# POOL and SP bound to program order, a head's loads placed nearer to their use, and two last splits on DVE

## The chip, the cores and the metric

The kernel runs on one core of a Trainium2 chip. The metric is device time in microseconds of one execution. The engines are named as in the profile: PE is TensorE (PEld its weight loads), DVE is VectorE, ACT is ScalarE, POOL is GpSimd, and SP is the engine that issues nearly all DMAs here.

## The reference

One transformer block over 2048 rows of width 576: an adaptive layer norm, attention with 32 query heads over 16 key and value heads (only the last 512 cached positions count, no mask inside them), a gated residual, a second adaptive layer norm, a SwiGLU MLP of width 4608, and a second gated residual. Cut to its core:

```python
mod = (_silu(c) @ w_mod).reshape(c.shape[0], 6, 1, -1)        # sa, ca, ga, sb, cb, gb
h = _layernorm(x) * (1 + ca) + sa
q = (h @ wq).reshape(B, Sq, Hq, Dh)...                         # 32 heads of 128
k = jnp.repeat(k_cache[:, :, Sk - W:, :], rep, axis=1)         # W = 512
v = jnp.repeat(v_cache[:, :, Sk - W:, :], rep, axis=1)
p = _softmax(jnp.einsum("bhqd,bhkd->bhqk", q, k) * Dh ** -0.5)
x = x + ga * (jnp.einsum("bhqk,bhkd->bhqd", p, v)... @ wo)
h = _layernorm(x) * (1 + cb) + sb
x = x + gb * ((_silu(h @ w1) * (h @ w3)) @ w2)
```

## The kernel before

Every float32 operand of a large product is split into a high part, rounded to the matmul's input type, and a low part, the difference. `split(hi, lo, src, eng)` does it: ACT casts (L84), then the engine `eng`, POOL or DVE, subtracts (L85). A product is then three matmuls: high by high, high by low, low by high. This split is what ACT, DVE and POOL spend much of their time on.

**Attention.** The 2048 rows form four blocks of 512. A *slot* is one head on one block; there are 128 slots, blocks 0 and 1 first, head by head, then blocks 2 and 3. The main loop runs over slots `i`, and inside over four *steps* `t`, each for 128 rows. In step t of loop i PE transposes the probabilities of slot i-1 (`turn`), makes the scores of slot i (`scores`), a quarter of the query projection of slot i+1 (`query`), and the output projection of slot i-2 (`attend_out`). After the four steps come the value products of slot i-1 (`values`). ACT takes the exponentials (L325), copies the transposed probabilities out (L336) and casts; DVE takes maxima (L319) and low halves and accumulates (L366).

**Side work during attention.** The loop calls `run(i, t)` at the end of each step (and `run(i, -1)` at the start of a slot); it emits the tasks that `at(i, t, task, ...)` registered. Those of a head: load wq (`load_in`), split it (`split_in`), load wo (`load_out`), multiply it by the gate on POOL (`gate`, L770), split it (`split_out`), load k (`load_kv`), transpose it on PE (`turn_k`), load v, split it (`split_v`). The loads of a head share a ring of three buffers with the tag `raw`. Also in these steps the weights of the MLP are prepared for a seven-product scheme (Strassen-like, ORDER and DOWN): `load_raw` (12 DMA issues, L471 and L474) and `make_set` (seven pieces per chunk f: ACT casts, L489; POOL subtracts, L490 and L491; SP stores to `wd`, L492; at n = 0 and n = 2 POOL first forms sums, L483 to L487), and `load_rows` and `make_rows` for w2. `make_rows` at n = 0 forms all the sums of a pair of row chunks on POOL, then makes its first piece out of the last of them:

```python
nc.gpsimd.tensor_mul(r, r, half_split(gates["b"]))      # L538, twice
nc.gpsimd.tensor_sub(t1, b12, b11)                      # L541
nc.gpsimd.tensor_sub(t2, b22, t1)                       # L542
nc.gpsimd.tensor_sub(t4, b21, t2)                       # L543
nc.gpsimd.tensor_sub(b12, b22, b12)                     # L544
k, x = (("p4", t4), ("p7", b12), ("p6", t2), ...)[n]
keep(x, ...)   # ACT cast L525, POOL subtraction L526, SP store to od L529
```

The prepared pieces pass through four buffers with the tag `xn`, each free again when its store has landed. There are 385 such items: 290 of them over the 232 steps of the list `early` (five items on four steps), the rest over the 128 steps of `late`. 19 of the items are `make_rows` at n = 0.

**MLP.** 72 groups (36 chunks f, each for two pairs of blocks) of seven products (`product`, L567), each with seven matmuls. `act_steps` splits the activations of a chunk pair between the products, and `down` multiplies them by the prepared rows (L645). In the last group, `plain` does four plain products per row tile instead; it needs the halves of p1 and p7, which `act_steps` splits at k = 0 and 1, and those of p4 and p2 at the end. `finish` adds partial sums on POOL (L589 to L593), `finish_first` (L600) on POOL or DVE.

**What sets the order.** Every engine executes its own queue in order. The framework's scheduler makes the queues: `tc.manual_schedule(engines=ORDERED)` keeps, for the engines in the set, the order in which the program emits its instructions; the others are ordered by the scheduler, which may move an instruction ahead of others on its engine when its inputs allow. Before, PE, DVE and ACT are in the set.

Of the kernel before, what the change touches and what calls it, by code (L numbers as in the profile page):

```python
# [24 lines left out]
HQ, HKV, DH = 32, 16, 128  # L25
# [5 lines left out]
EPS = 1e-5  # L31
PB, QB, RB, HB = 4, 1, 3, 7

ORDERED = {mybir.EngineType.PE, mybir.EngineType.DVE, mybir.EngineType.Activation}
SCALE = float(DH) ** -0.5


# [1 line left out]
def tile_block(  # L39
# [14 lines left out]
    nc = tc.nc  # L54
# [27 lines left out]
    def split(hi, lo, src, eng):  # L82

        nc.scalar.copy(hi, src)  # L84
        eng.tensor_sub(lo, src, hi.bitcast(F32))  # L85
# [210 lines left out]
    hT, wqs, keys, vals, wos = {}, {}, {}, {}, {}  # L296
# [277 lines left out]
    def split_act(d, k, x, eng):  # L574
        tags = ("ah", "al") if k in ("p7", "p4", "p6") else ("kv", "kv")
        hi, lo = [pool.tile([P, SB], F32R, tag=t, name=f"a{t}", bufs=8 if t == "kv" else 3) for t in tags]
        split(hi, lo, x, eng)
        halves[d, k] = hi, lo
# [82 lines left out]
    def act_steps(g, k):  # L661

        d, j = divmod(g, 2)
        x, pool_sub = acts[d], nc.gpsimd.tensor_sub
        if d == 2 * G - 1 and j == 1:
            if k in (0, 1):
                split_act(d, ("p1", "p7")[k], x[0, k], nc.gpsimd)
            elif k in (5, 6):
                split_act(d, ("p4", "p2")[k - 5], x[1, 6 - k], nc.vector)
        elif j == 0 and d and k < 4:  # L670
            o = acts[d - 1]
            if k == 0:
                split_act(d - 1, "p6", o[0, 0], nc.gpsimd)
            elif k == 1:
                split_act(d - 1, "p5", o[0, 1], nc.gpsimd)
            elif k == 2:
                split_act(d - 1, "p2", o[1, 0], nc.gpsimd)
                pool_sub(o[1, 0], o[1, 0], o[0, 0])
            elif k == 3:
                split_act(d - 1, "p3", o[1, 0], nc.gpsimd)  # L680
                del acts[d - 1]
        elif j == 1:
            if k == 0:
                x["s3"] = pool.tile([P, SB], F32, tag="ql", name="s3", bufs=QB)
                pool_sub(x["s3"], x[0, 0], x[0, 1])
            elif k == 1:
                split_act(d, "p7", x.pop("s3"), nc.gpsimd)
            elif k == 4:
                split_act(d, "p1", x[0, 0], nc.gpsimd)
            elif k == 5:  # L690
                split_act(d, "p4", x[1, 1], nc.vector)
            elif k == 6:
                nc.gpsimd.tensor_add(x[0, 1], x[0, 1], x[1, 1])
                pool_sub(x[0, 0], x[0, 1], x[0, 0])
# [6 lines left out]
    def mlp():  # L701

        for g in range(len(groups)):
# [9 lines left out]
            for k, name in enumerate(ORDER):  # L713
# [25 lines left out]
                elif name == "p4":  # L739
                    nc.vector.tensor_add(u0, st["x"], u0)  # L740
                    nc.vector.tensor_mul(u0, u0, st["s0"])
                act_steps(g, k)
                for _ in range(after[k]):
                    for task, *args in units:
# [9 lines left out]
    def at(i, t, task, *args):  # L754

        tasks.setdefault((i, t), []).append((task, args))
# [18 lines left out]
    for key, i in first.items():  # L775
        h, kv = key[1], (key[0], key[1] // 2)
        if i >= 2:
            at(i - 3, -1, load, wqs, key, load_in, wq, h * DH)
            at(i - 2, 1, put, wqs, key, split_in)
        at(max(i - 2, 0), -1, load, wos, key, load_out, wo, h * DH)  # L780
        at(max(i - 2, 1), 1, gate, wos, key, "a")
        at(max(i - 1, 1), 2, put, wos, key, split_out)
        if i and h % 2 == 0:
            at(i - 4, -1, load, keys, kv, load_kv, k_cache, h // 2)
            at(i - 2, -1, put, keys, kv, turn_k)
            at(i - 2, -1, load, vals, kv, load_kv, v_cache, h // 2)
            at(i - 1, 0, put, vals, kv, split_v)


# [91 lines left out]
    for c in range(3):  # L881
        i = 2 * HQ + 22 + 8 * c
# [141 lines left out]
```

## Time and profile before

| | us |
|---|---|
| median of 3 runs | 3106.66 (3104.28 to 3110.09) |
| the profiled execution | 3104.6 |
| its span in the profile | 3102.8 |
| PE busy | 3041.2 (98%) |
| DVE busy | 1997.0 (64%) |
| POOL busy | 1636.6 (53%) |
| ACT busy | 1483.0 (48%) |

Attention takes the first 1840 us or so of the span, with its side work densest from 170 to 800 us; the MLP the rest. In rows of the timeline the columns are the start, the time it took, the engine and line, the operation, what it writes and reads, the shapes, and, in brackets, the idle time of the engine before it and what ended that. Rows of the list of waits give the total us, the number of waits and the longest. Rows of DMA issues give the size of each and the median us from issue to landing. "SPq" is a DMA issue on SP's queue.

### The profile page before, as it was taken

The numbers are of one execution on the slowest core, as the hardware profiler recorded it, in microseconds if no ns is written. First come the engines' busy times: TensorE is split into PE (matmuls) and PEld (weight loads), VectorE is DVE, ScalarE is ACT, GpSimd is POOL, SyncE is SP. The second block draws the span as 40 slices with busy tenths as digits, with TensorE's granted clock in tenths as the row PEclk, the third lists the DMA queues.
The fourth block names the chain that finished last, engine by engine and source line by source line (L and its number), as shares of the span: only waits on it lengthen the run. The fifth ranks groups of instructions, "written<-read, shape, count | busy, mean of one in ns | idle before, by whom it ended". The sixth has DMA issues, their size and how long they took to land.

```text
span 3102.8 us, 48015 instructions
## 1 busy us (share of the span) xinstructions
PE 3041.2 (98%) x16948; PEld 2658.2 (86%) x16948; DVE 1997.0 (64%) x3039; ACT 1483.0 (48%) x3107; POOL 1636.6 (53%) x1659
## 2 busy tenths in 40 slices
PE   7999999999999999999999999999999999999998
PEld 6888888888888888888888888888888888888887
DVE  6767766676776777777777766555555555555555
ACT  4566666665666665566665553333333222322321
POOL 4278768777734742466773103355564353433434
PEclk8999999999999999999999999999999999999999
DMA  6145555554512532354444135677766766666663
GB/s 201 57 162 188 180 168 170 177 187 160 180 49 82 168 121 63 105 170 165 163 139 150 41 130 176 207 229 246 248 218 216 281 228 194 202 204 194 200 208 116
DMA packets 330128, 523.13 MB, mean 169 GB/s; under 512 B 32800, under 2 KB 161824, under 8 KB 328096
## 3 DMA queue, kind: packets, MB, share of 16 engines
q1 hardware_dynamic: 329280, 520.06, 50.9%
q8 instruction: 135, 2.21, 0.3%
q14 instruction: 105, 0.86, 0.1%
q10 hardware_dynamic: 608, 0.00, 0.0%
HBM read 369.76 MB, written 150.18 MB: 168 GB/s over the span
## 4 chain that ended last, share of the span: by engine, by line
PE 79%; POOL 9%; DMA 4%; SPq 2%; DVE 2%; issue 2%; ACT 1%; POOLq 0%; ACTq 0%; DVEq 0%
PE py L567 14%; PE px L567 10%; PE pe L282 10%; PE pq L266 8%; PE pf L645 6%; PE pe L645 6%; PE pt L335 5%; PE po L353 3%; PE po L352 3%; PE po L351 3%; PE pss L317 3%; PE pss L315 3%; PE pss L316 3%; PE pq L274 1%; SPq L474 1%
## 5 line engine op out<-in xcount | busy, mean ns | idle before, releaser
L325 ACT ACTIVATE p<-pss,nm 128x512 f32<-128x512 f32 x512 | 352.8, 689 | 348.4 <-DVE nm L319 347.5
L567 PE MATMUL py<-hset,wset 128*128 128x512 f32 x2016 | 509.0, 392 | 2.4 <-ACT u L733 2.1
L366 DVE SCALAR_TENSOR_TENSOR acc<-pe,r,acc 128x576 f32<-128x576 f32 x512 | 416.6, 814 | 49.9 <-PE pe L282 44.5
L319 DVE TENSOR_REDUCE nm<-pss 128x1 f32<-128x512 f32 x512 | 349.3, 682 | 113.2 <-PE pss L317 112.8
L567 PEld LDWEIGHTS py<-hset,wset 128*128 128x128 f32 x2016 | 363.3, 188 | 63.2 <-ACT u L733 3.6
L567 PE MATMUL px<-hset,wset 128*128 128x512 f32 x1512 | 381.5, 392 | 0.0
L282 PEld LDWEIGHTS pe<-o,oth 128*128 128x128 f32 x2048 | 326.7, 188 | 61.1 <-DVE acc L366 14.4
L342 DVE TENSOR_TENSOR ptl<-pt,pth 128x512 fp32r<-128x512 f32 x512 | 349.1, 682 | 39.9 <-ACT pth L336 39.0
L282 PE MATMUL pe<-o,oth 128*128 128x288 f32 x2048 | 358.0, 297 | 11.1 <-DVE acc L366 7.3
L567 PEld LDWEIGHTS px<-hset,wset 128*128 128x128 f32 x1512 | 276.5, 188 | 49.6
L336 ACT CAST pth<-pt 128x512 fp32r<-128x512 f32 x512 | 300.8, 588 | 35.4 <-PE pt L335 32.4
L335 PE MATMUL pt<-ident,p 128*128 128x128 f32 x2048 | 308.1, 273 | 4.9 <-DVE ptl L342 2.6
L85 POOL TENSOR_TENSOR akv<-u,akv 128x512 fp32r<-128x512 f32 x141 | 182.3, 1294 | 223.3 <-ACT akv L84 220.7
L335 PEld LDWEIGHTS pt<-ident,p 128*128 128x128 f32 x2048 | 249.8, 141 | 19.4 <-issue 3.0
L315 PE MATMUL pss<-kh,qh 128*128 128x512 f32 x512 | 245.3, 479 | 0.7 <-ACT qh L84 0.7
L85 DVE TENSOR_TENSOR otl<-po,oth 128x512 fp32r<-128x512 f32 x128 | 88.6, 692 | 243.1 <-ACT oth L84 243.1
L282 PE MATMUL pe<-o,otl 128*128 128x288 f32 x1024 | 219.7, 295 | 0.0
L490 POOL TENSOR_TENSOR wmade<-wraw,wmade 128x256 fp32r<-128x256 f32 x252 | 186.2, 739 | 45.9 <-ACT wmade L489 20.1
L266 PE MATMUL pq<-hT,wl 128*128 128x512 f32 x508 | 201.5, 397 | 8.5 <-POOL wl L85 5.7
L317 PE MATMUL pss<-kh,ql 128*128 128x512 f32 x512 | 203.2, 397 | 0.0
L316 PE MATMUL pss<-kl,qh 128*128 128x512 f32 x512 | 202.8, 396 | 0.0
L353 PE MATMUL po<-ptl,vh 128*128 128x512 f32 x512 | 201.1, 393 | 1.1 <-DVE ptl L342 1.1
(178 smaller groups left out, 6402.6 us busy)
## 6 DMA issues: line engine op xcount, KB each, us to landing
oset<-od SPq DMA_DIRECT2D x106, 576.0 KB, 4.9
od<-omade SPq DMA_DIRECT2D x133, 288.0 KB, 2.7
oraw<-in_A_wo SPq DMA_DIRECT2D x64, 288.0 KB, 2.8
wraw<-in_B_w SPq DMA_DIRECT2D x144, 128.0 KB, 2.6
wraw<-in_A_wq SPq DMA_DIRECT2D x64, 256.0 KB, 2.9
w2raw<-in_B_w SPq DMA_DIRECT2D x38, 288.0 KB, 3.4
oset<-od SPq DMA_DIRECT2D x35, 288.0 KB, 3.2
wraw<-in_B_w SPq DMA_DIRECT2D x288, 32.0 KB, 2.1
```

Source lines behind the costliest of these rows:

```text
L266: nc.tensor.matmul(ps, (wh if k < 2 else wl)[:, m, :], hT[DC + m if k == 1 else m], start=s == 0, stop=False,)
L282: nc.tensor.matmul(E[:, h, :HALF], a[:, rows], b[:, h * HALF : (h + 1) * HALF], start=n == 0, stop=n == 2)
L315: nc.tensor.matmul(pss, st["qh"][:, rows], kh, start=True, stop=False)
L317: nc.tensor.matmul(pss, st["ql"][:, rows], kh, start=False, stop=True)
L319: nc.vector.tensor_reduce(nm, pss, axis=AX.X, op=ALU.max, negate=True)
L325: nc.scalar.activation(p, pss, AF.Exp, bias=nm, accum_out=st["l"][:, t : t + 1])
L335: nc.tensor.transpose(ps[:, j, :], p[:, j * P : (j + 1) * P], ident)
L336: nc.scalar.copy(st["pt"][0][:, :, t * P : (t + 1) * P], ps)
L342: nc.vector.tensor_sub(pt[1][:, :, cols], state[i]["t"], pt[0][:, :, cols].bitcast(F32))
L366: nc.vector.scalar_tensor_tensor(a, E[:, :, :HALF], st["r"][:, t : t + 1], a, op0=ALU.mult, op1=ALU.add)
L567: nc.tensor.matmul(ps, w[:, a, :], h[:, b, :], start=start and n == 0, stop=stop and n == 6, skip_group_check=True)
L645: nc.tensor.matmul(ps[:, h, :HALF], a[:, rows], w[:, b, :], start=m == 0, stop=m == 2)
```

## The change

Three edits. POOL and SP join the set of engines that keep program order. In the last group of the MLP the low halves of p1 and p7 are subtracted on DVE instead of POOL. And for heads after the first ones the loads are registered at later steps: wq from the start of slot i-3 to the end of its step 1, wo from the start of slot i-2 to the end of its step 1, its gate from step 1 of slot i-2 to step 0 of slot i-1, k from the start of slot i-4 to step 0 of slot i-3, and v from the start of slot i-2 to the end of its step 0. The splits and the transposition stay where they are.

```diff
-ORDERED = {mybir.EngineType.PE, mybir.EngineType.DVE, mybir.EngineType.Activation}
+ORDERED = {mybir.EngineType.PE, mybir.EngineType.DVE, mybir.EngineType.Activation, mybir.EngineType.Pool, mybir.EngineType.SP}
...
         if d == 2 * G - 1 and j == 1:
             if k in (0, 1):
-                split_act(d, ("p1", "p7")[k], x[0, k], nc.gpsimd)
+                split_act(d, ("p1", "p7")[k], x[0, k], nc.vector)
...
         if i >= 2:
-            at(i - 3, -1, load, wqs, key, load_in, wq, h * DH)
+            at(i - 3, 1, load, wqs, key, load_in, wq, h * DH)
             at(i - 2, 1, put, wqs, key, split_in)
-        at(max(i - 2, 0), -1, load, wos, key, load_out, wo, h * DH)
-        at(max(i - 2, 1), 1, gate, wos, key, "a")
+        at(*(i - 2, 1) if i > 2 else (0, -1), load, wos, key, load_out, wo, h * DH)
+        at(*(i - 1, 0) if i > 2 else (1, 1), gate, wos, key, "a")
         at(max(i - 1, 1), 2, put, wos, key, split_out)
         if i and h % 2 == 0:
-            at(i - 4, -1, load, keys, kv, load_kv, k_cache, h // 2)
+            at(i - 3, 0, load, keys, kv, load_kv, k_cache, h // 2)
             at(i - 2, -1, put, keys, kv, turn_k)
-            at(i - 2, -1, load, vals, kv, load_kv, v_cache, h // 2)
+            at(i - 2, 0, load, vals, kv, load_kv, v_cache, h // 2)
             at(i - 1, 0, put, vals, kv, split_v)
```

## The prediction

> **What bounds the kernel now.** I read the page's header first, then the busy time of each engine stage by stage (columns: stretch, its length, busy us and instructions of PE, PEld, DVE, ACT, POOL, then granted clock, DMA share, GB/s).
>
> ```profile
> span 3102.8 us, 48015 instructions
> PE 3041.2 (98%) x16948; PEld 2658.2 (86%) x16948; DVE 1997.0 (64%) x3039; ACT 1483.0 (48%) x3107; POOL 1636.6 (53%) x1659
> 0.00:100.00 100.00, 81.55 (x410) 66.94 (x411) 70.51 (x119) 49.74 (x96) 38.41 (x40) 0.90 0.51 162
> 100.00:900.00 800.00, 778.89 (x4397) 673.34 (x4396) 553.47 (x880) 489.70 (x1111) 559.48 (x675) 0.99 0.49 161
> 900.00:1800.00 900.00, 899.08 (x5165) 789.90 (x5164) 643.71 (x1024) 538.98 (x1192) 472.05 (x497) 1.00 0.36 120
> 1800.00:3050.00 1250.00, 1242.63 (x6766) 1093.74 (x6765) 704.20 (x983) 397.56 (x698) 539.71 (x420) 1.00 0.65 212
> 3050.00:3103.00 53.00, 39.10 (x217) 34.25 (x215) 25.13 (x35) 7.06 (x12) 26.99 (x28) 0.94 0.25 87
> ```
>
> TensorE (PE) sets the time, and its order and its work stay as they are. Only its stops and its slow-clock stretches can change: 18.5 us idle in the first 100 us, 21.1 in 100 to 900, 0.9 in 900 to 1800, 7.4 in the long MLP stretch, 13.9 at the end. In 100 to 900 the clock share of 0.99 is about 8 us more. So no change off TensorE gains more than some 70 us; a loss has no such limit.
>
> **The end: two low halves go from POOL to DVE.** The timeline of the last group:
>
> ```profile
> 3037.85 1.23 DVE L85 TENSOR_TENSOR aal<-u,aah 128x512 fp32r<-128x512 f32 x1 [0.69 <-ACT aah L84]
> 3063.78 0.62 ACT L84 CAST akv<-u 128x512 fp32r<-128x512 f32 x1
> 3069.39 0.79 POOL L593 TENSOR_TENSOR sums<-sums 128x288 f32<-128x288 f32 x1
> 3070.14 1.26 POOL L85 TENSOR_TENSOR akv<-u,akv 128x512 fp32r<-128x512 f32 x1
> 3071.46 1.33 PE L645 MATMUL pf<-oset,akv 128*128 128x288 f32 x4 [6.40 <-POOL akv L85]
> 3085.92 0.69 DVE L85 TENSOR_TENSOR aal<-u,aah 128x512 fp32r<-128x512 f32 x1 [0.69 <-ACT aah L84]
> 3071.40:3076.00 4.60, 4.54 (x14) 3.87 (x15) 0.76 (x1) 0.14 (x1) 2.34 (x3) 0.52 0.00 0
> ```
>
> ACT has the high half of p1 at 3064.40, but POOL first ends the sums of `finish` (L593 to 3070.18), so the low half comes at 3071.40 and TensorE waits 6.40 us; then the clock stands at 0.52 for 4.54 busy us, another 2.2. On DVE the subtraction takes 0.69 (or 1.23 beside POOL): ready by 3065.1 to 3065.6, leaving 0.1 to 0.7 us of wait. Gain 5.7 to 8.5, taken as 8. The `finish` chain ends as before at 3070.2, the additions of `finish_first` behind it are wanted only by the last products, and DVE is near idle here (0.76 us in the last row), so the gain reaches the end. A rule speaks against it: the Trainium skill, "SBUF — State Buffer", section "SBUF: two separate sides", has a DVE operation with two SBUF inputs and a POOL operation that reads SBUF lock each other out for a whole instruction. The 1.23 against 0.69 above agrees; by the rule each of the two subtractions may wait out one 0.79 us addition, and the gain would be nearer 8 - 2 x 0.79 = 6.4.
>
> **POOL in program order: the chain of `make_rows`.** For each pair of down rows, `make_rows` at k = 0 emits on POOL two multiplications (L538) and L541, L542, L543, L544, and in the same step `keep` emits ACT's cast (L525) of t4, which L543 makes. ACT already keeps program order. Now POOL is free to run ahead, and does:
>
> ```profile
> 403.06 1.44 POOL L538 TENSOR_TENSOR w2raw<-w2raw,gate_b 128x576 f32<-128x576 f32 x1 [5.01 <-DMA w2raw<-in_B_w]
> 404.57 0.81 POOL L541 TENSOR_TENSOR w2raw<-w2raw 128x288 f32<-128x288 f32 x1
> 405.34 1.45 POOL L538 TENSOR_TENSOR w2raw<-w2raw,gate_b 128x576 f32<-128x576 f32 x1
> 406.86 0.81 POOL L542 TENSOR_TENSOR w2raw<-w2raw 128x288 f32<-128x288 f32 x1
> 407.63 0.81 POOL L544 TENSOR_TENSOR w2raw<-w2raw 128x288 f32<-128x288 f32 x1
> 408.40 0.81 POOL L543 TENSOR_TENSOR w2raw<-w2raw 128x288 f32<-128x288 f32 x1
> 434.40 0.66 ACT L84 CAST o<-oraw 128x576 fp32r<-128x576 f32 x1
> 434.96 0.43 ACT L525 CAST omade<-w2raw 128x288 fp32r<-128x288 f32 x1
> L538 POOL TENSOR_TENSOR w2raw<-w2raw,gate_b 128x576 f32<-128x576 f32 x38 | 54.4, 1433 | 34.7 <-DMA w2raw<-in_B_w 34.5
> L85 POOL TENSOR_TENSOR o<-oraw,o 128x576 fp32r<-128x576 f32 x61 | 87.6, 1436 | 105.5 <-ACT o L84 95.0 <-issue 8.8 <-POOL wmade L491 0.9
> ```
>
> The chain was done at 409.2, the cast came at 434.96 and found it ready. In program order POOL may not begin it before what stands ahead in its queue, here the low half of `o` (L85), which waits for ACT's own cast of `o` (to 435.06). So: 435.06 + 1.43 (o) + 2 x 1.51 (starts of L538 to its successor) + 2 x 0.77 + 0.81 = 441.9, and ACT, free for L525 at 435.0, stands 6.9 us, with every exp and pt cast behind it. If POOL comes to this point with work of its own left, it is more (8.5 here: a gate, a v split and three wmade pairs stand in the two steps before). Where nothing stands right ahead, POOL starts up to 1 us early: 4.4 to 5.4. There are 19 chains (38 of L538). Adding row durations for each in program order, against ACT's times in this execution: 12 wait 6.6 to 8.5, five 4.4 to 6.4, two next to nothing; 114 us together, 6.7 each over the 17.
>
> What a standing ACT costs TensorE, this trace shows where ACT waits for a store to free one of its four `xn` buffers:
>
> ```profile
> 199.14 0.43 ACT L525 CAST omade<-w2raw 128x288 fp32r<-128x288 f32 x1 [4.06 <-DMA wd1p<-wmade]
> 412.70 0.51 ACT L489 CAST wmade<-wraw 128x384 fp32r<-128x384 f32 x1 [6.00 <-DMA wd8p<-wmade]
> 472.19 0.51 ACT L489 CAST wmade<-wraw 128x384 fp32r<-128x384 f32 x1 [5.18 <-DMA wd10p<-wmade]
> 716.74 0.51 ACT L489 CAST wmade<-wraw 128x384 fp32r<-128x384 f32 x1 [4.88 <-DMA wd18p<-wmade]
> 778.04 0.51 ACT L489 CAST wmade<-wraw 128x384 fp32r<-128x384 f32 x1 [6.98 <-DMA wd20p<-wmade]
> 194.00:204.00 10.00, 9.46 (x53) 7.85 (x53) 5.07 (x9) 4.10 (x10) 9.37 (x13) 1.00 0.37 135
> 408.70:418.70 10.00, 7.64 (x45) 6.00 (x44) 4.74 (x9) 4.96 (x12) 8.98 (x14) 1.00 0.43 159
> 470.00:480.00 10.00, 8.56 (x41) 6.88 (x39) 5.47 (x9) 5.44 (x12) 8.60 (x12) 0.83 0.43 161
> 712.70:722.70 10.00, 7.67 (x46) 6.43 (x45) 4.07 (x7) 3.18 (x7) 9.21 (x14) 1.00 0.44 160
> 774.00:786.00 12.00, 7.60 (x30) 6.34 (x29) 3.63 (x7) 4.38 (x10) 11.14 (x16) 0.72 0.46 166
> ```
>
> Idle plus busy time x (1 - clock): 4.06 of ACT cost 0.5, 6.00 cost 2.4, 5.18 cost 2.9, 4.88 cost 2.3, 6.98 cost 6.5. So 0.5 to 3.6 us of a wait is covered, by the second score bank and the p tiles that ACT has filled ahead. Read as "wait less 2.24" (mean of the four long ones) the chains cost 113.8 - 17 x 2.24 = 76. By the nearest row, 12 x 6.5 + 5 x 2.6 = 91. I take 83; ends 54 (3.5 us covered each time) and 114 (nothing covered).
>
> **What program order gives back.** The stops of the last fence arise because POOL's hoisted work stood between a cast and its low half, so stores left late. Without hoisting the halves follow their casts sooner, and a wl no longer queues behind work that nobody needs yet. The stage holds 21 + 8 = 29 us of such loss: between 0 and 29 goes, I take 15. New ones appear right behind a chain, since its store (SP) waits for it with later stores behind; I set those at 0 to +10 and take 0, since ACT then stands anyway.
>
> **SP in program order, and later loads.** A head's wq load moves two steps later (`i - 3, 1`), its wo load and gate about as far (`i - 2, 1`; `i - 1, 0`), v one, and k a whole slot (from `i - 4, -1` to `i - 3, 0`), ahead of PE's own transposes at `i - 2, -1`. K is the tightest: three steps and the values matmuls.
>
> ```profile
> 437.36 0.39 PE L351 MATMUL po<-pth,vh 128*128 128x512 f32 x1
> 440.11 0.60 PE L335 MATMUL pt<-ident,p 128*128 128x128 f32 x4
> 442.74 0.60 PE L335 MATMUL pt<-ident,p 128*128 128x128 f32 x4
> kvraw<-in_A_k_cache SPq DMA_DIRECT2D x32, 256.0 KB, 2.9
> 448.51 1.88 SPq L474 DMA_DIRECT2D wraw<-in_B_w  x4
> SPq L492 <- POOL wmade L491: 328.7, 204, 10.6
> ```
>
> A step is 2.63 us, the values 2.75: 3 x 2.63 + 2.75 = 10.6, less 2.9 to land, leaves SP 7.7 us of lateness before TensorE waits for a transpose. The wq and v loads have a slot (13.3), the wo load 10.6 to its gate. SP waited up to 10.6 us for one wmade low half already, and a `load_raw` holds it 12 x 0.47 = 5.6 us; both in front of one k load are rare, so I cost the moves at 0, cover that slack, with +17 as the upper end (three k loads 6 us late). Loads that the scheduler had pulled far ahead (x of blocks 2 and 3, w_mod) go back to their steps, a slot or more before use: 0, up to +2. In the MLP stretch weight sets are loaded a group (22 us) ahead, and POOL's splits already come in program order: 0, from -2 to +4. Startup keeps its order: 0.
>
> **Sum.** 3104.6 (the profiled execution: span 3102.8 and 1.8 around it; the median of the runs is 2.1 above it, so it stands for them within 0.1%) + 83 (chains) - 15 (old stops) - 8 (end) + 0 = 3164.6; I say 3165. Ends: 3104.6 + 54 - 29 - 8.5 = 3121, and 3104.6 + 114 + 10 + 17 - 5.7 = 3240.
>
> **The rivals.**
> Faster: POOL gets ahead of the chains anyway. Program order ties POOL to ACT only through low halves; where the last one stands more than 5.4 us before a chain, the chain is done in time, as at two of the 19. Then only the end and two thirds of the old stops move: 3104.6 - 8 - 20 = 3077. It decides if the mean wait falls under 3.6 us, where 17 x (3.6 - 2.24) = 23 is what the other terms give. Against it: in the early steps five items fall on four steps, so a low half nearly always stands within a step. 11%.
> Same: waits of 3 to 4 us, mostly covered as the 4.06 was (0.5): within 6 us of 3105. 4%.
> Slower still by SP: k loads late and ACT waiting 2 us more for a store after each chain: 3165 + 17 + 17 x 2 = 3216. For it, the 10.6 us above; against it, the slack of 7.7. 15%.
> Slower still by the clock: if every stop lets it drop, as the 6.98 one did and the 6.00 and 4.88 ones did not, each of the 17 costs 6.7 - 2.6 = 4.1 idle and 2.1 of slow clock: 105 instead of 83, 3187. 15%. The Trainium skill, "TensorE: Matmul & The Clock Gate", section "Part 1: The HAM clock gate", lets the clock fall to half after about one idle window of 3.4 us; 0.52 after the 6.40 us wait agrees, and 2.36 us of idle in 408.7 to 418.7 left 1.00.
> The change does not do what it says (POOL still ahead): the 11% covers it.
>
> **Numbers.** My forecast, 3121 to 3210, has 55%. Less than 0.2% (6 us) can hardly be told from no change here. Slower 85% (55 + 15 + 15), same 4%, faster 11%. Leaving out the faster and the same case and the far upper tail, the range is 3110 to 3222.
>
> **What would show it.** Right: `ACT omade L525 <- POOL w2raw L543` high in the list of waits, near 17 times and 6 to 8 us each, with otl and acc on DVE late behind it; TensorE idle in 100 to 900 above 21 us, and in 900 to 1800, near none now, some 20 to 30; L538 starting within 3 us of its cast instead of 32 before. At the end, no wait on akv, and a clock of 1.00 after it. Wrong: no ACT wait on L543, or such waits with TensorE busy through them; `PE pt L252 <- DMA kvraw` would say SP.

## The result and the profile after

The changed kernel takes 3181.74 us (median; 3181.14 to 3186.68) against 3108.38 for the one before, measured beside it: a ratio of the means of 1.0241, interval 1.0224 to 1.0259. It is slower by 73 us by the medians and 75 by the ratio; 60 were forecast, and the time lies inside the range of 3110 to 3222.

The page's header for the changed kernel, and behind it its busy time by stretches, columns as before:

```profile
span 3179.2 us, 47924 instructions
PE 3060.5 (96%) x16948; PEld 2677.0 (84%) x16948; DVE 1998.4 (63%) x3041; ACT 1484.4 (47%) x3107; POOL 1635.0 (51%) x1657
```

```profile
0.00:100.00 100.00, 80.78 (x416) 66.07 (x417) 71.06 (x121) 50.99 (x98) 34.56 (x36) 0.93 0.43 132
100.00:900.00 800.00, 751.74 (x4188) 653.63 (x4187) 524.57 (x833) 468.74 (x1066) 555.58 (x670) 0.97 0.50 162
900.00:1800.00 900.00, 869.29 (x4931) 762.19 (x4930) 615.75 (x984) 519.72 (x1149) 463.44 (x495) 0.98 0.36 117
1800.00:3050.00 1250.00, 1238.63 (x6751) 1089.24 (x6750) 710.83 (x1002) 412.96 (x743) 521.34 (x405) 1.00 0.61 203
```

DVE, ACT and POOL are busy as long as before, to 2 us. TensorE's idle time grew from 21.1 to 48.3 us in 100 to 900 and from 0.9 to 30.7 in 900 to 1800: 57 us more. The clock fell there to 0.97 and 0.98, and with the same matmuls TensorE is busy 19 us longer (3060.5 against 3041.2). So nearly all of the loss is in the stage where the side work runs. The list of waits names what holds ACT, and through it DVE and TensorE (total us, number, longest):

```profile
ACT omade L525 <- POOL w2raw L543: 106.6, 18, 7.6
...
DVE ptl L342 <- ACT pth L336: 103.4, 49, 8.5
...
PE pe L282 <- DVE acc L366: 60.1, 15, 7.2
...
PE po L351 <- ACT pth L336: 13.7, 4, 5.5
```

The first row did not exist before, and the second and the third were these:

```profile
DVE ptl L342 <- ACT pth L336: 39.0, 47, 2.6
...
PE pe L282 <- DVE acc L366: 7.3, 11, 1.7
```

Here is the chain that the prediction worked out by hand, in the timeline of the changed kernel:

```profile
451.57 0.66 ACT L84 CAST o<-oraw 128x576 fp32r<-128x576 f32 x1
452.57 1.44 POOL L85 TENSOR_TENSOR o<-oraw,o 128x576 fp32r<-128x576 f32 x1
...
453.96 2.77 POOL L538 TENSOR_TENSOR w2raw<-w2raw,gate_b 128x576 f32<-128x576 f32 x2
...
454.28 0.43 PE L282 MATMUL pe<-o,otl 128*128 128x288 f32 x2
...
458.43 0.79 POOL L543 TENSOR_TENSOR w2raw<-w2raw 128x288 f32<-128x288 f32 x1
...
459.25 0.43 ACT L525 CAST omade<-w2raw 128x288 fp32r<-128x288 f32 x1 [7.02 <-POOL w2raw L543]
...
460.20 0.69 DVE L342 TENSOR_TENSOR ptl<-pt,pth 128x512 fp32r<-128x512 f32 x1 [6.71 <-ACT pth L336]
460.22 0.80 PE L351 MATMUL po<-pth,vh 128*128 128x512 f32 x1 [5.51 <-ACT pth L336]
```

The stretches of ten us around it, in the changed kernel:

```profile
450.00:460.00 10.00, 4.70 (x28) 3.98 (x26) 2.80 (x4) 2.14 (x6) 9.53 (x12) 0.93 0.39 132
460.00:470.00 10.00, 9.78 (x39) 7.99 (x40) 5.39 (x9) 4.65 (x12) 2.62 (x4) 0.72 0.46 138
```

ACT is free at 452.2 and stands 7.02 us while POOL (9.53 of 10 us busy) does the low half of `o`, both multiplications and the three subtractions. The next step's pt copy waits behind the cast, so DVE waits 6.71 us and TensorE 5.51. At other chains it is DVE's accumulation L366 that comes late, and with it TensorE's next output projection (L282): the row of 60.1 us in the list above. Then the clock runs at 0.72 for ten us. The first stretch says how completely TensorE stood: 28 matmuls, where the kernel before runs 55 in a mean ten us (4397 in 800).

At the end of the kernel the other edit did what it says:

```profile
3147.63 0.62 ACT L84 CAST akv<-u 128x512 fp32r<-128x512 f32 x1
...
3148.29 1.17 DVE L85 TENSOR_TENSOR akv<-u,akv 128x512 fp32r<-128x512 f32 x1 [1.24 <-ACT akv L84]
...
3149.52 0.80 PE L645 MATMUL pf<-oset,akv 128*128 128x288 f32 x4 [0.60 <-DVE akv L85]
```

The wait of 6.40 us is 0.60, near the upper end of the 0.1 to 0.7 forecast: the subtraction took 1.17 us beside POOL and not 0.69.

### The profile page after: what moved, and what is told of

The parts are those of the page before. It is cut to its first block, busy times and chain, and to the rows that moved or that the text cites. A ratio compares the mean times of both kernels' runs of the same rounds, so it can differ in the third digit from the quotient of the medians.

```text
span 3179.2 us, 47924 instructions
## 1 busy us (share of the span) xinstructions
PE 3060.5 (96%) x16948; PEld 2677.0 (84%) x16948; DVE 1998.4 (63%) x3041; ACT 1484.4 (47%) x3107; POOL 1635.0 (51%) x1657
## 4 chain that ended last, share of the span: by engine, by line
PE 75%; POOL 8%; issue 3%; DVE 2%; ACT 2%; DMA 1%; SPq 0%; POOLq 0%; ACTq 0%; DVEq 0%
PE py L567 13%; PE px L567 10%; PE pe L282 10%; PE pq L266 8%; PE pf L645 6%; PE pe L645 6%; PE pt L335 5%; PE po L351 3%; PE po L352 3%; PE po L353 3%; PE pss L315 3%; PE pss L317 3%; PE pss L316 3%; PE pq L274 1%; POOL w2raw L538 1%
## 5 line engine op out<-in xcount | busy, mean ns | idle before, releaser
L567 PE MATMUL py<-hset,wset 128*128 128x512 f32 x2016 | 509.3, 392 | 6.8 <-ACT u L733 6.7
L366 DVE SCALAR_TENSOR_TENSOR acc<-pe,r,acc 128x576 f32<-128x576 f32 x512 | 416.7, 814 | 52.1 <-PE pe L282 46.6
L282 PEld LDWEIGHTS pe<-o,oth 128*128 128x128 f32 x2048 | 331.2, 191 | 116.3 <-DVE acc L366 68.2
L282 PE MATMUL pe<-o,oth 128*128 128x288 f32 x2048 | 363.5, 300 | 65.6 <-DVE acc L366 60.1
L567 PEld LDWEIGHTS py<-hset,wset 128*128 128x128 f32 x2016 | 363.3, 188 | 68.3 <-ACT u L733 8.6
L567 PE MATMUL px<-hset,wset 128*128 128x512 f32 x1512 | 381.0, 391 | 0.0
L567 PEld LDWEIGHTS px<-hset,wset 128*128 128x128 f32 x1512 | 276.4, 188 | 49.7
L282 PE MATMUL pe<-o,otl 128*128 128x288 f32 x1024 | 222.0, 298 | 0.0
L351 PE MATMUL po<-pth,vh 128*128 128x512 f32 x512 | 204.4, 399 | 13.7 <-ACT pth L336 13.7
L84 ACT CAST oth<-po 128x512 fp32r<-128x512 f32 x128 | 75.1, 586 | 303.3 <-PE po L353 303.3
L352 PE MATMUL po<-pth,vl 128*128 128x512 f32 x512 | 204.2, 399 | 0.0
```

What stands on the lines that cost most here:

```text
L282: nc.tensor.matmul(E[:, h, :HALF], a[:, rows], b[:, h * HALF : (h + 1) * HALF], start=n == 0, stop=n == 2)
L351: nc.tensor.matmul(po, vh[:, j, :], pt[0][:, j, :], start=j == 0, stop=False)
L366: nc.vector.scalar_tensor_tensor(a, E[:, :, :HALF], st["r"][:, t : t + 1], a, op0=ALU.mult, op1=ALU.add)
L567: nc.tensor.matmul(ps, w[:, a, :], h[:, b, :], start=start and n == 0, stop=stop and n == 6, skip_group_check=True)
```

## Experiments

Two theories were on trial first. The chain theory: ACT stands for the first cast of `make_rows`, and that is the loss. The rival: SP in program order, or loads too close to their use. Times are medians; ratios are of means, to the kernel before on the same chip, and one thousandth is 3.1 us. Differences between kernels go by the ratios.

**Which queue.** Two kernels give one of the queues back to the scheduler.

```diff
-ORDERED = {..., mybir.EngineType.Pool, mybir.EngineType.SP}
+ORDERED = {..., mybir.EngineType.SP}        # e3: POOL free
+ORDERED = {..., mybir.EngineType.Pool}      # e4: SP free
```

> The changed kernel, but POOL may again be ordered by the scheduler; SP keeps program order and the loads stay late. Chain theory: the scheduler pulls the chain far ahead as before, no ACT wait on L543, 3085 to 3110 us. Rival (SP order or late loads): stays at 3165 to 3185.

> The changed kernel, but SP may again be ordered by the scheduler; POOL keeps program order. Chain theory: nothing changes for the 18 waits, 3170 to 3190 us. Rival (SP order): falls to 3085 to 3110.

With POOL free: 3086.71 us, 0.9942 (0.9926 to 0.9959). With SP free: 3183.28, 1.0255 (1.0237 to 1.0274), and the wait is unchanged (list of waits of that kernel):

```profile
ACT omade L525 <- POOL w2raw L543: 106.8, 18, 7.6
```

So POOL's program order costs 93 us (1.0241 less 0.9942). SP's, beside it, costs nothing. And without POOL in the set, the change would have made the kernel faster by 0.6%.

**Is it the chain?** Two cures leave POOL and SP in program order. One emits the six POOL operations ahead of the cast, two or four steps; with four, the rows are loaded eight steps ahead instead of six. The other leaves POOL's queue alone and changes which piece ACT casts first.

```diff
# e1, e8: as a task of its own, 2 or 4 steps before make_rows(p, 0)
+    def sum_rows(p):                 # L538 twice, L541, L542, L543, L544
+ at((step - 2) // 4, (step - 2) % 4, sum_rows, w)
# e2: only the two multiplications (L538) two steps ahead
# e10: the order of the pieces
-    (("p4", t4), ("p7", b12), ("p6", t2), ("p1", b11), ("p5", t1), ("p2", b21), ("p3", b22))[n]
+    (("p1", b11), ("p2", b21), ("p3", b22), ("p5", t1), ("p6", t2), ("p7", b12), ("p4", t4))[n]
```

> The changed kernel with one thing moved: the two multiplications and four subtractions of a pair of down rows are emitted two steps before the first piece is cast (same work, same engine, POOL and SP still in program order). Chain theory (ACT stands at the cast of t4 until POOL has made it): ACT's wait on L543 falls from 106.6 us to under 10, TensorE's idle time in 900 to 1800 from 31 us to under 3, and the kernel takes 3075 to 3105 us. Rival (SP in program order, or loads too close to their use, cost the time): 3165 to 3185, since neither is touched.

Measured: 3109.81 us, 1.0016 (1.0007 to 1.0025). 70 of the 75 us come back, so the rival falls. But 900 to 1800 kept 4.9 us of idle time, not under 3, the time is above the expected 3105, and ACT still waits on POOL for t4 (its subtraction is L542 in that kernel's numbering), and for stores to free its buffers. From the list of waits:

```profile
ACT omade L525 <- POOL w2raw L542: 25.5, 9, 4.3
...
ACT omade L525 <- DMA od<-omade: 33.4, 13, 4.5
```

> Only the two multiplications of the chain are emitted two steps earlier; the four subtractions stay with the cast. Chain theory: each of the 18 waits gets about 3.0 us shorter (106.6 to some 53 us together, 2.9 each), and since the first 0.5 to 3.6 us of an ACT wait were covered before, most of the loss goes: 3090 to 3125 us. If a wait were not covered at all and TensorE lost what ACT waits, only 54 us would come back: about 3128. Rival (SP or loads): 3165 to 3185.

A miss: 3156.53 us, 1.0161 (1.0139 to 1.0182). ACT's wait fell by 22 us, not by some 53. Its list of waits (L546 there is the subtraction that makes t4):

```profile
ACT omade L525 <- POOL w2raw L546: 84.4, 18, 7.0
```

And POOL's timeline at the same chain, which says why:

```profile
439.82 0.46 POOL L491 TENSOR_TENSOR wmade<-wraw,wmade 64x128 fp32r<-64x128 f32 x1
440.36 2.83 POOL L535 TENSOR_TENSOR w2raw<-w2raw,gate_b 128x576 f32<-128x576 f32 x2
443.14 0.74 POOL L490 TENSOR_TENSOR wmade<-wraw,wmade 128x256 fp32r<-128x256 f32 x1
...
444.49 1.40 POOL L85 TENSOR_TENSOR o<-oraw,o 128x576 fp32r<-128x576 f32 x1
...
447.58 0.79 POOL L546 TENSOR_TENSOR w2raw<-w2raw 128x288 f32<-128x288 f32 x1
```

The rows follow each other without a gap. POOL was full before the chain too, so the multiplications moved ahead only push back the low halves between them and the cast: `o` starts at 444.49, and here ACT waits 7.05 us as ever. On a full queue it does not help to move work that stands ahead of t4 further ahead, since t4 comes after all of it either way; with the sums ahead t4 itself was emitted earlier. 22.2 us of ACT's wait went, and 25 us of time. These two are not from the same execution: the profiled one, which has the waits, is the fastest of four (3146.36), 35 us below the profiled one of the changed kernel.

> The changed kernel with the seven pieces of a pair of down rows cast in another order: b11, b21, b22, t1, t2, b12, t4. POOL's chain keeps its place and length (7 us of work in one step), but ACT's first cast needs only the first multiplication. Chain theory (it is ACT's wait that costs): each of the 18 waits gets 3.9 us shorter (1.51 + 3 x 0.8 of the chain no longer stand before it), 106.6 to about 36 us, nearly all covered: 3090 to 3115 us. Rival (POOL's 7 us burst itself costs, by making low halves such as wl late): 3150 to 3180.

Measured: 3109.42 us, 1.0016 (1.0007 to 1.0025), with POOL's burst where it was.

```profile
ACT omade L525 <- POOL w2raw L538: 42.1, 18, 3.7
```

The wait fell by 64.5 us and the time by 70. So it is ACT's standing and not the burst on POOL. What is left, 2.3 us each, costs little: with both cures (below) it costs at most 7 us.

> As the kernel with the sums two steps ahead, but four steps ahead, and the rows loaded eight steps ahead instead of six. There, 25.5 us of ACT waits on L542 in 9 of the chains were left. If these are the rest of the loss, they go and the time is 3085 to 3098 us; if program order on POOL costs elsewhere (the MLP stretch kept 11.3 us of TensorE idle time against 7.7 with POOL free), it stays at 3098 to 3108.

3106.09 us, 1.0003 (0.9994 to 1.0012): the second of the two outcomes. Then both cures together:

> Both queues in program order, sums four steps ahead and t4 cast last, the two cures together. Each alone came out at 3106 to 3109. If ACT's remaining waits on POOL are all that is left in attention, they vanish and 3092 to 3100 comes out, with the 4 us that the MLP stretch loses in program order; if stores behind POOL's burst hold ACT instead (34 us of waits on od with the sums ahead), it stays at 3103 to 3109.

3102.71 us, 0.9996 (0.9988 to 1.0005): between the two outcomes, just below the 3103 to 3109 of the second and above the 3092 to 3100 of the first. Against the kernel with POOL free, 17 us stay (0.9996 less 0.9942). Two stretches of that kernel, then the same of the one with both cures:

```profile
100.00:900.00 800.00, 786.48 (x4475) 683.80 (x4474) 563.11 (x894) 498.83 (x1128) 570.07 (x683) 1.00 0.51 166
...
1800.00:3050.00 1250.00, 1242.27 (x6766) 1094.04 (x6765) 703.55 (x980) 393.83 (x689) 546.18 (x428) 1.00 0.64 215
```

```profile
100.00:900.00 800.00, 779.91 (x4417) 675.10 (x4416) 554.18 (x882) 492.48 (x1117) 569.14 (x682) 1.00 0.50 165
...
1800.00:3050.00 1250.00, 1237.49 (x6725) 1088.67 (x6723) 700.28 (x978) 395.23 (x694) 537.93 (x418) 1.00 0.63 212
```

And rows of the lists of waits, in the same order (L567 and L571 are the product of the MLP, L733 and L737 the copy of u1):

```profile
ACT omade L525 <- DMA od<-omade: 20.6, 12, 3.2
...
PE py L567 <- ACT u L733: 2.2, 3, 1.2
```

```profile
ACT omade L525 <- DMA od<-omade: 32.1, 15, 5.0
...
PE py L571 <- ACT u L737: 6.6, 7, 2.4
```

About 7 us of idle time are in 100 to 900 and 5 in the MLP stretch, where ACT is late with the copy of a product; TensorE is also busy 5 us longer over the whole kernel (3039.3 against 3034.5). In 100 to 900 ACT waits longer for stores of `od`, but less for those of `wd`: 54 us for all stores over 100 to 1800, against 50 with POOL free. So the stores alone do not explain the 7 us, and what does, there and in the MLP, was not tried apart.

**What SP's order and the late loads are worth.** Without POOL in the set the changed kernel is faster than the end alone explains. Four kernels, all with the DVE splits and POOL free, take the four corners.

```diff
# e5: the kernel before, with only  split_act(..., nc.vector)
# e9: late loads, SP free         # e13: old loads, SP in order
# e3: late loads, SP in order
```

> The kernel before with one edit: the low halves of p1 and p7 in the last group go to DVE. Prediction's term for the end: 5.7 to 8.5 us less, 3096 to 3099 against 3104 to 3105 (ratio 0.9973 to 0.9982). If the two subtractions wait out POOL's additions on the port that DVE and POOL share, 1.6 us less of that. Rival (the gain is given back before the end, since the last sums are late next): ratio 0.999 to 1.001.

> The changed kernel with POOL and SP both left to the scheduler again, so that only the late loads and the DVE splits remain. The kernel with SP in order and POOL free came out at 0.9942, some 10 us below what the end alone gives. If the later loads gave those 10 us, this one is at 0.993 to 0.996 too; if SP's program order gave them, it is at 0.997 to 0.999, the end's gain alone.

> SP in program order, POOL free, loads at their old steps: the missing corner of four (SP free and early loads 3098, SP free and late loads 3124, SP in order and late loads 3087). If SP's order alone is what helps, this is near 3087 (3082 to 3092); if late loads and SP's order help only together, since a load emitted early holds an SP in program order until a raw buffer comes free, 3095 to 3125.

| POOL free, DVE splits | loads as before | loads late |
|---|---|---|
| SP free | 3098.32, 0.9981 (0.9972 to 0.9990) | 3123.62, 1.0059 (1.0047 to 1.0072) |
| SP in order | 3121.66, 1.0052 (1.0039 to 1.0064) | 3086.71, 0.9942 (0.9926 to 0.9959) |

The end alone gives 5.9 us (3 to 9). The expectation for both queues free missed altogether: neither the loads nor the order gives the 12 us further; each alone costs 22 to 24 us, and only both together gain. Most of the loss lies in attention. The stretch from 100 to 900, first with only the end changed, then with the loads late and SP free, then with the old loads and SP in order:

```profile
100.00:900.00 800.00, 781.04 (x4415) 675.35 (x4414) 554.58 (x882) 492.66 (x1115) 562.79 (x678) 1.00 0.49 161
```

```profile
100.00:900.00 800.00, 764.32 (x4247) 656.02 (x4246) 530.78 (x847) 474.91 (x1079) 552.29 (x667) 0.99 0.48 159
```

```profile
100.00:900.00 800.00, 769.33 (x4302) 662.57 (x4303) 539.35 (x859) 479.62 (x1086) 559.01 (x673) 0.99 0.50 166
```

TensorE is idle 19.0, 35.7 and 30.7 us there (13.5 with both edits, shown above), and the two bad corners have a clock of 0.99. POOL's wait for the wo loads is longest in the two bad corners. From the lists of waits over 100 to 1800: only the end, loads late alone, SP in order alone, and both:

```profile
POOL oraw L770 <- DMA oraw<-in_A_wo: 62.1, 31, 4.0
```

```profile
POOL oraw L770 <- DMA oraw<-in_A_wo: 142.4, 32, 20.6
```

```profile
POOL oraw L770 <- DMA oraw<-in_A_wo: 108.6, 35, 4.5
```

```profile
POOL oraw L770 <- DMA oraw<-in_A_wo: 70.2, 24, 7.8
```

So are ACT's waits for stores to free its buffers, added over the same stretch: 85, 130, 93 and 50 us. That fits a POOL that the scheduler has lined up behind a gate whose load is not there yet, so that low halves, and the stores after them, are late. Whether the gate's wait is the cause or a companion, no run took apart.

The same move of the loads with both queues in program order:

> The changed kernel (POOL and SP in program order) with the loads of a head back at their old steps. Chain theory, and the prediction's 0 for the moves: the 18 waits on L543 stay at 105 to 110 us and the time at 3170 to 3195. Rival (loads placed late are part of the loss): 3150 to 3170. Third way (SP in program order with early loads holds SP at the ring of three raw buffers): above 3195.

3196.10 us, 1.0296 (1.0280 to 1.0311), the third of the three ways by 1 us; the wait on the chain is longer too:

```profile
ACT omade L525 <- POOL w2raw L543: 116.4, 18, 8.4
```

So placing the loads late gains 17 us in the changed kernel. That SP is held at the ring of raw buffers does not explain it by itself. SP's waits at the three lines that load into the ring (over 100 to 1800) are 219 us here and 166 in the changed kernel; but with both queues free late loads shorten them by about as much, from 544 to 498 us, and there they lose 24 us.

**The fastest.**

> The fastest kernel so far (SP in order, POOL free, late loads, DVE splits) with t4 cast last. There ACT still waits some 25 us for stores and 15 us for POOL, and TensorE idles 13.5 us in 100 to 900. If POOL's hoisting of the chain is what still makes stores late, a chain that is wanted later is hoisted no less by the scheduler, and nothing changes (3082 to 3092); if the cast order matters, 3075 to 3082.

3086.10 us, 0.9938 (0.9926 to 0.9950): as without the new cast order. Both kernels with POOL free and SP in order beat the one before by 0.6% and the changed one by 3%.

## Why the prediction was right, and where it was off

The measured steps follow the runs, so that they add up by construction: the end (0.9981), then SP's order with the late loads (0.9942), then POOL's order with both cures (0.9996), then the chains uncured (1.0241).

| term | forecast, us | measured, us |
|---|---|---|
| chains of `make_rows` | +83 (54 to 114) | +76 |
| POOL's order elsewhere: old stops given back | -15 (0 to -29) | +17 with the next two |
| new stops behind a chain | 0 (0 to +10) | |
| MLP | 0 (-2 to +4) | |
| SP's order and the moves of loads | 0 (up to +17) | -12 |
| end | -8 (5.7 to 8.5) | -5.9 (3 to 9) |
| sum | +60 | +75 |

The chains carry the result, and they were understood. That the sum came so near is in part luck: POOL's order elsewhere was off by 32 us one way, SP and the loads by 12 and the chains by 7 the other, and the first two lie outside their stated bounds.

**The chains.** Right in mechanism, count and length. 18 waits of 106.6 us against 17 with 114 worked out; the one worked by hand at 8.5 us (6.9 without other work ahead) came out at 7.02. The two chains said to wait next to nothing are one that is done in time and one with little wait. The price per us was read well too: "wait less 2.24" on the measured list gives 106.6 - 18 x 2.24 = 66, the nearest rows of the prediction's waits about 78; 70 (with the new cast order) to 76 (with both cures) came back. Of an ACT wait the first 2.3 us or so are nearly free (the new cast order left that much at each chain), and beyond that each us cost 1.1 on average (64.5 us of wait, 70 of time). In the two profiled executions 50 us of these are idle time of TensorE and 20 are longer busy time at the lower clock, like the 0.72 in the stretch after the chain shown. The rival of the clock at every stop (3187) lies within 6 us of the time, but the sum reaches 3182 another way: its 105 for the chains is not what the cures gave back.

**The old stops.** This step failed: POOL's order is not shown to give anything back. In the changed kernel ACT's waits for stores do shrink, to 4.6 us against 85 in the kernel with only the end changed (added over 100 to 1800). But where the chains are cured, with POOL still in program order, they return: 24 us with the new cast order, 39 with the sums two steps ahead, 54 with both cures, against 50 with POOL free. So the 4.6 go with an ACT that already stands at the chains. What was gained, 12 us, came with POOL free, from SP's order with the late loads, and neither of the two alone gains it; that it is near the 15 is luck.

**SP and the loads.** "I cost the moves at 0" failed. With SP in order late loads gain 34 us if POOL is free and 17 if it is not; with both free they lose 24. The bounds came from the distance to use (7.7 us of slack for k) and left out that the place of a load acts together with the order of the queues; by what path stays open. The prediction's rival of late k loads did not show: the list of waits has one wait of TensorE for a k load, 1.1 us in the first 100 us, and it was 0.7 before.

**POOL's order elsewhere.** The step "0, from -2 to +4" for the MLP was at its edge: 11.4 us idle there against 7.4, 4 more. In attention 7 us more idle time than with POOL free stay when the chains are cured; the prediction had "0 to +10" for late stores and took 0. These and the 5 us of longer busy time are the 17 us as far as the profiles place them; their cause stays open. A gain of 15 was forecast where this loss came.

**The end.** The wait went from 6.40 to 0.60 us, and the clock in the 4.5 us after it from 0.52 to 1.00 (a stretch of the changed kernel):

```profile
3149.50:3154.00 4.50, 4.48 (x24) 3.95 (x25) 2.96 (x4) 1.73 (x3) 4.19 (x6) 1.00 0.00 0
```

Alone it measured 5.9, with an interval that holds both the 8 and the 6.4 of the prediction's rule, so the time cannot choose between them. The Trainium skill's rule for the lock between DVE and POOL ("SBUF — State Buffer", section "SBUF: two separate sides") agrees with the 1.17 us that the subtraction took beside POOL's additions, against 0.69.

## What to carry to other kernels

Before an engine is put into program order, look for its results that an in-order engine asks for in the very step that emits them: a chain of POOL work right before ACT's cast was harmless because the scheduler had it done some 26 us early. Either emit the whole chain ahead, its last result with it (two steps gave back 70 of 75 us; moving only its first part on a full queue gave 25), or let the consumer take first the piece that is ready first, which cost one line and gave back 70 too. Test orders of queues and places of loads together: here each of two edits alone lost 22 to 24 us and both together won 12.

## What was not expected of the hardware

A TensorE stop can cost more than itself, through a slower clock after it, and its length alone did not decide whether. In the timeline of the kernel before, these are the stops that followed the waits of 6.00, 5.18 and 4.88 us in the prediction:

```profile
413.75 0.54 PE L282 MATMUL pe<-o,oth 128*128 128x288 f32 x2 [2.24 <-ACT oth L84]
...
473.24 0.80 PE L282 MATMUL pe<-o,oth 128*128 128x288 f32 x4 [1.31 <-ACT oth L84]
...
718.45 0.50 PE L266 MATMUL pq<-hT,wl 128*128 128x512 f32 x1 [2.33 <-DVE otl L85]
```

In the ten us around the first and the third the granted clock was 1.00. Over the ten us after the 5.51 us stop of the changed kernel it was 0.72, with 9.78 busy: 2.7 us lost. The Trainium skill, "TensorE: Matmul & The Clock Gate", section "Part 1: The HAM clock gate", puts the drop at an idle window of about 3.4 us, and the stops of 2.24, 2.33 and 5.51 us lie on both sides of that as it says. The second row differs: after a stop of 1.31 us the clock was 0.71 from 474 to 476 and 0.50 from 476 to 478, with 1.00 before (0.83 over the ten us). So a slow clock followed a stop well under 3.4 us too, which the prediction's rival of the clock left aside, and no run here shows why.
